# The transposes of the first expert's late token chunks, listed ahead of the third early second-pass chunk

## The chip, the cores and the metric

One core of one Trainium2 chip runs one launch of the kernel. The metric is device time in microseconds (us), the median of the timed runs of the whole launch. TensorE (PE in the rows) does matrix products, VectorE (DVE) and ScalarE (ACT) evict and split results, GpSimd (POOL) subtracts and issues gathers and scatters by index, SyncE (SP) issues the other loads. Each engine takes its instructions in the order of a list of its own, and the five lists wait for each other by semaphores.

## What is computed

```python
def reference(**kwargs):
    attn_out = _attn_ref(q, k, v)          # block-causal attention, 4 x 8 heads, 576 tokens, head size 64
    x = attn_out as 2304 tokens x 512
    x = _moe_ref(x, w1, w2, w3, w_out)     # max of three products, then one product back to 512
    return _moe2_ref(x, ...)               # 8 experts, the two best of each token

def _moe2_ref(x, w_gate, w_noise, noise, w1, w2):
    ...
    for e in range(E):
        for k in range(2):
            mask = top2[:, k] == e
            h = np.maximum(x[mask] @ w1[e], 0.0)
            out[mask] += top2_w[mask, k, None] * (h @ w2[e])
```

## The kernel before, in words

Attention and the first mixture layer fill the first half of the launch. This case lies in the second half, the eight experts. Every number is kept as a high and a low fp32r part, and a product takes three matmuls: high by high, low by high, high by low.

The tokens of an expert are packed into up to five chunks of 128 (chunks 0 to 4). For an expert `e` the steps are:

- `gather(e)`: one indirect DMA on POOL for each chunk brings 128 rows of `x2d` into a tile `xg` (L1078; 6 buffers, so a later gather waits until the transposes have read an earlier tile).
- `transposes(e, c0, c1)`: four transposes on PE for each chunk (L1096) into one PSUM bank, then ACT copies the bank to the high part `xh` (L1098) and DVE subtracts for the low part `xl` (L1099).
- `mm1(e, f, ...)`, the first pass: for each of 8 groups `f` of 128 hidden columns, four blocks of the depth by three matmuls (L1108 to L1110) into one PSUM bank; ACT evicts the high part (L1112), DVE the low part (L1113).
- `mm2(e, c, HT)`, the second pass: for each chunk 8 groups by three matmuls (L1156 to L1158); DVE scales the result into `y` (L1161, for the first expert L1163), and POOL scatters `y` to `out_rows` (L1164).

The weights of the next expert come in six pieces (`load_expert`): SP loads a piece into `rw` (2 buffers; L159 or L164), ACT copies the high part to `w` (L172), POOL subtracts the low part (L173). The subtraction is what gives `rw` back, so the load of piece 3 waits for the subtraction of piece 1, and so on.

The first expert is split. Its chunks 0 to 2 (`CE = 3`) are known early: they are transposed and pass `mm1` in 8 groups of 384 tokens while the last tokens are still being routed. Chunks 3 and 4 are gathered after that, and the program then lists the second pass of chunks 0, 1 and 2, the transposes of chunks 3 and 4, their `mm1` (8 groups of 256 tokens, 96 matmuls), the second pass of chunk 3, the five transposes of the next expert, the second pass of chunk 4, and then expert by expert. The banks of the transposes and of both passes come from `bank2()`, which takes a `b` and a `t` bank in turn, four buffers each.

The order on each engine is not the program's: a scheduler places the instructions by a simulated time line, and among those ready it goes by the place in the program. So ACT's list mixes the copies of weight pieces (L172), of transposes (L1098) and the evictions (L1112), and one that waits holds all that stand behind it.

Of the kernel before, what the change touches and what calls it, by code (L numbers as in the profile page):

```python
# [29 lines left out]
CE = 3  # L30
# [80 lines left out]
def plain(ap):  # L111
    return ap.bitcast(F32)
# [3 lines left out]
def tile_attention_moe_moe(ctx, tc, qT, kT, v, w1, w2, w3, w_out, gates, noise, e1, e2, out):  # L116
# [938 lines left out]
    def bank2():  # L1055
        turn[0] ^= 1
        if turn[0]:
            return ps2.tile([128, 512], F32, name="b")
        return psT.tile([128, 512], F32, name="t", bufs=4)
# [6 lines left out]
    def wt2(e, s, f):  # L1066
        g = f // 3
        o = (f - 3 * g) * 512
        return EW[e, 1, g][:, s, o:o + 512]
# [13 lines left out]
    def transposes(e, c0=0, c1=NCH):  # L1083
        if c0 == 0:
            XGT[e] = [mw.tile([128, 4, CAP], F32R, name=n) for n in ("xh", "xl")]
        th, tl = XGT[e]
        for c in range(c0, c1):
            if e == 0 and c < CE and BT:
                ps = ps2.tile([128, 512], F32, name="b")
            else:  # L1090
                ps = bank2()
            ps = ps.rearrange("p (k t) -> p k t", k=4)
            n = min(128, CAPS[e] - 128 * c)
            ps = ps[:, :, :n]
            for kt in range(4):
                nc.tensor.transpose(ps[:, kt], XG[e, c][:n, kt * 128:(kt + 1) * 128], ident[:n, :n])  # L1096
            s = slice(c * 128, c * 128 + n)
            nc.scalar.activation(th[:, :, s], ps, AF.Copy)  # L1098
            nc.vector.tensor_sub(tl[:, :, s], ps, plain(th[:, :, s]))  # L1099
# [39 lines left out]
    def mm2(e, c, HT):  # L1139
        n = min(128, CAPS[e] - 128 * c)  # L1140
        at, by = isc[:n, e, c:c + 1], idt[:n, e, c, 1:2]
        if e == 0 and c < CE:
            at, by = ise[:n, c:c + 1], ide[0][:n, c, 1:2]
        if e:
            prev = PREV[(e * NCH + c) % 2][:n]
            gi = nc.gpsimd.indirect_dma_start(
                out=prev, out_offset=None, in_=out,
                in_offset=bass.IndirectOffsetOnAxis(ap=at, axis=0),
                bounds_check=NTOK - 1, oob_is_err=False)
            for (ee, o) in osc:  # L1150
                if ee == e:
                    tc.declare_no_dep(gi.ins, o.ins, reason="rows of other tokens")
        ps = bank2()[:n]
        for f in range(8):
            a, l = (HT[f](s, c * 128, c * 128 + n) for s in range(2))
            nc.tensor.matmul(ps, a, wt2(e, 0, f), start=f == 0, stop=False)  # L1156
            nc.tensor.matmul(ps, a, wt2(e, 1, f), start=False, stop=False)  # L1157
            nc.tensor.matmul(ps, l, wt2(e, 0, f), start=False, stop=f == 7)  # L1158
        y = mw.tile([128, DM], F32, name="y", bufs=2)[:n]
        if e:  # L1160
            nc.vector.scalar_tensor_tensor(y, ps, by, prev, op0=OP.mult, op1=OP.add)  # L1161
        else:
            nc.vector.tensor_scalar(y, ps, by, None, op0=OP.mult)  # L1163
        st = nc.gpsimd.indirect_dma_start(  # L1164
            out=out, out_offset=bass.IndirectOffsetOnAxis(ap=at, axis=0),
            in_=y, in_offset=None, bounds_check=NTOK - 1, oob_is_err=False)
        for (ee, o) in osc:
            if ee == e:
                tc.declare_no_dep(st.ins, o.ins, reason="rows of other tokens")
        osc.append((e, st))  # L1170
# [86 lines left out]
    nc.vector.tensor_scalar(ig[:, 1:], idt[:, 1:, :, 0], float(NTOK - 1), None, op0=OP.min)  # L1257
    nc.vector.tensor_copy(isc[:, 1:], idt[:, 1:, :, 0])
    for c in range(CE):
        mm2(0, c, HT)  # L1260
    transposes(0, CE)
    for e in range(E):
        nw = weights_of(e + 1) if e + 1 < E else iter(())
        if e == 1:
# [121 lines left out]
```

## Time and profile before

| | |
|---|---|
| median of 3 runs | 1006.35 us (1005.23 to 1008.45) |
| the profiled execution, its own time | 1008.53 us |
| its span, first to last instruction | 1006.8 us |
| mean granted TensorE clock | 0.988 |
| PE busy | 978.2 us (97%) |
| DVE, ACT, POOL busy | 430.0, 398.1, 393.1 us |

The span is what the rows below are counted in, from its start; 1.73 us of the execution's time lie around it. The profiled execution is the slowest of the runs shown, 2.18 us above their median. PE is the busiest engine by far; the others have idle time of their own, which costs nothing as long as PE does not wait for it. In the rows, a group in square brackets at the end of a line is the idle time of the engine just before the instruction, and what ended it.

### The profile page before, as it was taken

How to read it: one execution, taken by the hardware profiler on the slowest of the kernel's cores; microseconds unless marked ns; L12 is line 12 of the kernel's file. 1: busy time of each engine (PE TensorE's matmuls, PEld its weight loads, DVE VectorE, ACT ScalarE, POOL GpSimd, SP SyncE). 2: the span in 40 equal slices, each digit the busy share in tenths (PEclk: the TensorE clock that was granted, in tenths of full speed). 3: DMA queues.
4: the chain of work that ended last, by engine and by line, in shares of the span. 5: the costliest groups of instructions: out<-in, count | busy, mean ns of one | idle time of the engine just before them, and what ended most of it. 6: DMA issues, size and time to landing. Idle time of an engine off the chain costs nothing. (4 is left out here: it accounts for less than half of the span.)

```text
span 1006.8 us, 17057 instructions
## 1 busy us (share of the span) xinstructions
PE 978.2 (97%) x6558; PEld 875.3 (87%) x6558; DVE 430.0 (43%) x1260; ACT 398.1 (40%) x934; POOL 393.1 (39%) x303
## 2 busy tenths in 40 slices
PE   8989998999999999999999799999999999999997
PEld 5876897999999899999999699898898989888895
DVE  6873556664567665743246322222222222221221
ACT  5586444654545545541124144232332414232210
POOL 2875120130302213121221477574756556574302
PEclk9999998999999999999999999999999999999999
DMA  8831315122112121302013456353534445342101
GB/s 267 289 125 52 109 38 196 51 54 64 36 44 70 55 63 41 84 23 98 22 33 126 148 162 208 115 177 105 160 107 154 146 138 171 106 165 84 61 12 57
DMA packets 75860, 106.15 MB, mean 105 GB/s; under 512 B 23548, under 2 KB 48124, under 8 KB 75776
## 3 DMA queue, kind: packets, MB, share of 16 engines
q1 hardware_dynamic: 63408, 75.97, 24.3%
q0 software_dynamic: 10192, 28.28, 8.6%
q10 hardware_dynamic: 2176, 0.79, 0.4%
q8 instruction: 52, 0.85, 0.4%
q14 instruction: 32, 0.26, 0.1%
HBM read 85.35 MB, written 20.53 MB: 105 GB/s over the span
## 5 line engine op out<-in xcount | busy, mean ns | idle before, releaser
L173 POOL TENSOR_TENSOR w<-rw,w 128x1536 fp32r<-128x1536 f32 (+1 forms) x42 | 131.6, 3138 | 74.2 <-ACT w L172 57.6
L752 POOL TENSOR_TENSOR hl<-hm,hh 128x512 fp32r<-128x512 f32 x21 | 27.4, 1303 | 175.6 <-ACT hh L751 174.5
L172 ACT ACTIVATE w<-rw 128x1536 fp32r<-128x1536 f32 (+1 forms) x42 | 56.4, 1344 | 81.4 <-issue 43.3
L1108 PE MATMUL b<-xh,w 128*128 128x384 f32 (+7 forms) x272 | 87.9, 323 | 0.5 <-DVE xB L1113 0.5
L1110 PE MATMUL b<-xh,w 128*128 128x384 f32 (+7 forms) x272 | 87.6, 322 | 0.0
L1109 PE MATMUL b<-xl,w 128*128 128x384 f32 (+7 forms) x272 | 87.5, 322 | 0.0
L736 PE MATMUL t<-xA,w 128*128 128x256 f32 x288 | 83.6, 290 | 0.0
L737 PE MATMUL t<-xA,w 128*128 128x256 f32 x288 | 82.5, 287 | 0.0
L738 PE MATMUL t<-xA,w 128*128 128x256 f32 x288 | 82.2, 285 | 0.0
L1108 PE MATMUL t<-xh,w 128*128 128x256 f32 x240 | 68.4, 285 | 5.1 <-ACT xh L1098 5.1
L265 POOL TENSOR_TENSOR Kl<-rk,Kh 128x576 fp32r<-128x576 f32 x16 | 23.0, 1439 | 123.8 <-ACT Kh L264 123.8
L1164 POOL DMA_INDIRECT out_rows<-y,isc x37 | 37.4, 1012 | 81.1 <-DVE y L1161 77.1
L1113 DVE SCALAR_TENSOR_TENSOR ht<-b,ht 128x384 fp32r<-128x384 f32 (+6 forms) x56 | 29.1, 520 | 92.7 <-ACT ht L1112 92.6
L1109 PE MATMUL t<-xl,w 128*128 128x256 f32 x240 | 67.8, 283 | 0.0
L1110 PE MATMUL t<-xh,w 128*128 128x256 f32 x240 | 67.8, 283 | 0.0
L1156 PE MATMUL b<-w,ht 128*128 128x512 f32 (+1 forms) x168 | 67.0, 399 | 0.0
L1158 PE MATMUL b<-w,ht 128*128 128x512 f32 (+1 forms) x168 | 66.4, 395 | 0.0
L1157 PE MATMUL b<-w,ht 128*128 128x512 f32 (+1 forms) x168 | 66.3, 394 | 0.0
L925 POOL DMA_INDIRECT ids<-rows,slots x36 | 35.7, 992 | 72.6 <-DVE slots L922 64.4
L736 PE MATMUL t<-xB,w 128*128 128x256 f32 x216 | 61.8, 286 | 0.0
L737 PE MATMUL t<-xB,w 128*128 128x256 f32 x216 | 61.3, 284 | 0.0
L738 PE MATMUL t<-xB,w 128*128 128x256 f32 x216 | 61.1, 283 | 0.0
(396 smaller groups left out, 2787.4 us busy)
## 6 DMA issues: line engine op xcount, KB each, us to landing
rw<-in_e SPq DMA_DIRECT2D x32, 768.0 KB
w<-in_w SPq DMA_DIRECT2D x18, 512.0 KB
rw<-in_e SPq DMA_DIRECT2D x16, 512.0 KB
rk<-in_kT SPq DMA_DIRECT2D x16, 288.0 KB
x2d<-x SPq DMA_DIRECT2D x18, 256.0 KB
out_rows<-x SPq DMA_DIRECT2D x9, 512.0 KB
w<-in_w_out SPq DMA_DIRECT2D x6, 512.0 KB
rq<-in_qT SPq DMA_DIRECT2D x16, 160.0 KB
```

Of the source, the lines that this page charges most:

```text
L172: nc.scalar.activation(t[:, 0, :c], r[:, :c], AF.Copy)
L173: nc.gpsimd.tensor_sub(t[:, 1, :c], r[:, :c], plain(t[:, 0, :c]))
L736: nc.tensor.matmul(ps[:, j], wh, x[:, 0], start=kt == 0, stop=False)
L737: nc.tensor.matmul(ps[:, j], wh, x[:, 1], start=False, stop=False)
L738: nc.tensor.matmul(ps[:, j], wl, x[:, 0], start=False, stop=kt == 3)
L1108: nc.tensor.matmul(p, wt1(e, 0, kt, f), th[:, kt, c0:c1], start=kt == 0, stop=False)
L1109: nc.tensor.matmul(p, wt1(e, 0, kt, f), tl[:, kt, c0:c1], start=False, stop=False)
L1110: nc.tensor.matmul(p, wt1(e, 1, kt, f), th[:, kt, c0:c1], start=False, stop=kt == 3)
L1156: nc.tensor.matmul(ps, a, wt2(e, 0, f), start=f == 0, stop=False)
L1157: nc.tensor.matmul(ps, a, wt2(e, 1, f), start=False, stop=False)
L1158: nc.tensor.matmul(ps, l, wt2(e, 0, f), start=False, stop=f == 7)
L1164: st = nc.gpsimd.indirect_dma_start(out=out, out_offset=bass.IndirectOffsetOnAxis(ap=at, axis=0), in_=y, in_offset=None, bounds_check=NTOK ...
```

## The change

```diff
     for c in range(CE):
+        if c == CE - 1:
+            transposes(0, CE)
         mm2(0, c, HT)
-    transposes(0, CE)
     for e in range(E):
```

The transposes of the first expert's chunks 3 and 4 are listed between the second pass of chunk 1 and that of chunk 2. Nothing is added or removed. The scheduler then also places other instructions anew.

PE, at the end of the second pass of chunk 1 (its bank is `t`) and the start of that of chunk 2 (bank `b`, first operand in `xB`); lines with + are of the change:

```order
 L1157 MATMUL t<-w,hl 128x512
 L1158 MATMUL t<-w,hh 128x512
+L1096 MATMUL b<-ident,xg 128x128 x4
+L1096 MATMUL t<-ident,xg 128x128 x4
 L1156 MATMUL b<-w,xB 128x512
 L1157 MATMUL b<-w,xB 128x512
```

The eight transposes now stand ahead of the 24 matmuls of chunk 2; in the kernel before they stand behind them.

ACT, from the last evictions of the early `mm1` (into `hm` and `hl`, 128x384) on. The 128x256 rows of L1112 are the evictions of the late `mm1`, groups 0, 1, 2 and so on. Before:

```order
L1112 ACTIVATE hl<-b 128x384
L172 ACTIVATE w<-rw 128x1536
L1098 ACTIVATE xh<-t 128x4x128
L172 ACTIVATE w<-rw 128x1536
L1098 ACTIVATE xh<-b 128x4x128
L1112 ACTIVATE hl<-t 128x256
L1112 ACTIVATE hh<-b 128x256
L1112 ACTIVATE hl<-t 128x256
L172 ACTIVATE w<-rw 128x1024
```

And in the changed kernel, one row further on:

```order
L1098 ACTIVATE xh<-b 128x4x128
L1098 ACTIVATE xh<-t 128x4x128
L172 ACTIVATE w<-rw 128x1536 x2
L1112 ACTIVATE hl<-t 128x256
L1112 ACTIVATE hh<-b 128x256
L1112 ACTIVATE hl<-t 128x256
L1112 ACTIVATE hx<-b 128x256
L1112 ACTIVATE x_6884<-t 128x256
L1112 ACTIVATE hx<-b 128x256
L172 ACTIVATE w<-rw 128x1024
L1112 ACTIVATE x_6916<-t 128x256
L1112 ACTIVATE hx<-b 128x256
```

Both copies of transposes now stand ahead of the first two weight pieces, and weight piece 3 has moved from behind group 2 to behind group 5. In both kernels pieces 4 and 5 follow group 7, and then come the five transpose copies of the next expert.

POOL, from the gathers of chunks 3 and 4 (the first row) on; L173 is the subtraction of a weight piece:

```order
 L1078 DMA xg<-x2d,ig 128x512 x2
 L1164 DMA out_rows<-y,ise 2304x512 x2
-L1078 DMA xg<-x2d,ig 128x512 x4
-L173 TENSOR_TENSOR w<-rw,w 128x1536
-L1078 DMA xg<-x2d,ig 128x512
+L1078 DMA xg<-x2d,ig 128x512 x6
+L173 TENSOR_TENSOR w<-rw,w 128x1536
 L1164 DMA out_rows<-y,ise 2304x512
-L1078 DMA xg<-x2d,ig 128x512
```

Two gathers of later experts, which use the `xg` tiles of chunks 3 and 4 again, have moved from behind the subtraction of weight piece 1 to ahead of it. On DVE the low part of chunk 3 now stands ahead of, and that of chunk 4 behind, the conversion of the other experts' index lists (L1257).

## Rows read from the trace of the kernel before

**Rows 1.** Waits of PE over the whole span: us in total, times, longest us

```profile
PE t L1108 <- ACT xh L1098: 5.1, 1, 5.1
```

**Rows 2.** Time line of PE: start us, us, instruction, count, [idle before <- what ended it]

```profile
566.38 0.39 PE L1156 MATMUL b<-w,xB 128*128 128x512 f32 x1
...
571.98 0.60 PE L1096 MATMUL t<-ident,xg 128*128 128x128 f32 x4
572.42 0.60 PE L1096 MATMUL b<-ident,xg 128*128 128x128 f32 x4
578.07 0.58 PE L1108 MATMUL t<-xh,w 128*128 128x256 f32 x1 [5.05 <-ACT xh L1098]
...
582.49 0.28 PE L1108 MATMUL b<-xh,w 128*128 128x256 f32 x1
...
591.54 0.39 PE L1156 MATMUL t<-w,hl 128*128 128x512 f32 x1
...
604.92 0.34 PE L1108 MATMUL b<-xh,w 128*128 128x384 f32 x1
```

**Rows 3.** Busy time by stretch; PEclk, the granted clock, stands third from the end

```profile
578.00:582.00 4.00, 3.93 (x18) 3.93 (x19) 0.69 (x1) 0.02 (x1) 3.23 (x4) 0.50 0.37 124
...
583.00:591.00 8.00, 8.00 (x70) 8.00 (x69) 2.51 (x7) 3.23 (x7) 5.90 (x2) 1.00 0.61 158
```

**Rows 4.** Time line of ACT at the transposes

```profile
573.93 1.48 ACT L172 ACTIVATE w<-rw 128x1536 fp32r<-128x1536 f32 x1 [18.17 <-DMA rw<-in_e]
...
576.05 1.48 ACT L172 ACTIVATE w<-rw 128x1536 fp32r<-128x1536 f32 x1
577.44 0.58 ACT L1098 ACTIVATE xh<-b 128x512 fp32r<-128x512 f32 x1
```

**Rows 5.** Gather of chunk 4 on POOL, then a stretch; its last number is GB/s

```profile
559.48 0.96 POOL L1078 DMA_INDIRECT xg<-x2d,ig  x1 [0.30 <-issue]
...
559.00:563.00 4.00, 4.00 (x19) 3.23 (x18) 2.16 (x10) 0.00 (x0) 1.89 (x3) 1.00 0.48 132
```

**Rows 6.** Time line of DVE: the conversion of the index lists

```profile
570.58 0.18 DVE L1257 TENSOR_SCALAR ig<-idt 128x35 int32<-128x35 f32 x1 [3.24 <-DMA idt<-ids]
```

**Rows 7.** Time line of POOL: a gather and three weight subtractions

```profile
574.84 0.95 POOL L1078 DMA_INDIRECT xg<-x2d,ig  x1 [0.30 <-issue]
575.80 3.46 POOL L173 TENSOR_TENSOR w<-rw,w 128x1536 fp32r<-128x1536 f32 x1
...
582.98 3.55 POOL L173 TENSOR_TENSOR w<-rw,w 128x1536 fp32r<-128x1536 f32 x1
...
586.49 2.41 POOL L173 TENSOR_TENSOR w<-rw,w 128x1024 fp32r<-128x1024 f32 x1
```

**Rows 8.** Weight pieces 3, 5 and 9: issue on SP's queue, copy on ACT

```profile
579.29 0.37 SPq L159 DMA_DIRECT2D rw<-in_e  x1
585.36 1.06 ACT L172 ACTIVATE w<-rw 128x1024 fp32r<-128x1024 f32 x1
...
594.28 1.49 ACT L172 ACTIVATE w<-rw 128x1536 fp32r<-128x1536 f32 x1 [0.77 <-DMA rw<-in_e]
...
615.18 0.37 SPq L159 DMA_DIRECT2D rw<-in_e  x1
...
618.80 1.06 ACT L172 ACTIVATE w<-rw 128x1024 fp32r<-128x1024 f32 x1 [0.54 <-DMA rw<-in_e]
```

**Rows 9.** Second expert's transposes: first and third copy on ACT, third subtraction on DVE

```profile
597.78 0.60 ACT L1098 ACTIVATE xh<-b 128x512 fp32r<-128x512 f32 x1 [2.01 <-PE b L1096]
...
598.75 0.60 ACT L1098 ACTIVATE xh<-b 128x512 fp32r<-128x512 f32 x1
...
599.61 0.68 DVE L1099 TENSOR_TENSOR xl<-b,xh 128x512 fp32r<-128x512 f32 x1
```

**Rows 10.** Third expert: its fifth weight subtraction on POOL, its first eviction on ACT

```profile
635.28 3.50 POOL L173 TENSOR_TENSOR w<-rw,w 128x1536 fp32r<-128x1536 f32 x1 [3.39 <-ACT w L172]
...
665.59 0.48 ACT L1112 ACTIVATE ht<-b 128x368 fp32r<-128x368 f32 x1 [1.72 <-PE b L1110]
```

## The prediction

> **What bounds the kernel now.** I read the page first (PE is busy 97% of the span), then the list of PE's waits over the whole span, and then the time lines around the one wait that stands out. The longest single wait of PE lies exactly where the change works: once, for 5.1 us, the first matmuls of the late first pass wait for a transpose copy on ACT [rows 1]. From there to the last matmul of the launch the list names no other wait of PE. So after this point the launch is as long as PE's list, and whatever PE gains here reaches the end, if nothing else then becomes late.
>
> The time line of PE shows the place. The second pass of chunk 2 runs from 566.38 to 571.98 (24 matmuls, 5.6 us, 0.70 for a group of three), the eight transposes follow it, the last four starting at 572.42, and PE stands from 573.02 to 578.07 [rows 2]. ACT shows why. It has been idle for 18.17 us, held by a weight piece whose load lands at 573.93; only behind that copy comes the first transpose copy, and behind a second weight copy (576.05) the second one at 577.44, which ends at 578.02 [rows 4]. The transposes had been ready since 573. PE did not wait for the copies' work, but for two weight loads that stood ahead of them in ACT's list.
>
> The pause costs a second time. [...]
>
> **The change, part by part.**
>
> *PE's work.* The eight transposes are the same eight, ahead of chunk 2 instead of behind it, so chunk 2 and the transposes together still end at 573.0. Cost nothing.
>
> *The wait removed.* The transposes now run at 566.4 to 567.4, when ACT has nothing to do until 573.93 [rows 4]. Two copies of 0.58 us are over by about 568.5. On DVE the low part of chunk 3 follows at once; that of chunk 4 stands behind the conversion of index lists, which runs at 570.58 when its load lands [rows 6], and is ready about 571.5, with 0.18 for that conversion, as much for the one behind it, and 0.7 for the subtraction. Both are before 573.0, so the late first pass starts without the wait: **5.05 us** [rows 2]. Chunk 2's 5.6 us are the cover for copies and subtractions; without it PE would wait for at least the last copy and subtraction, 0.58 + 0.68 = 1.3.
>
> *The clock.* The late first pass is 8 groups of 12, 96 matmuls, and runs from 578.07 to 591.54, 13.47 us. Until 582.49 stand 20 of them, 0.221 us each; from there to 591.54 the last 76, 0.119 each [rows 2]. At 0.119 throughout it would take 11.43. With no pause ahead of it there is no reason for the fall, so **2.04 us** more. Together 7.09.
>
> *What is queued behind the moved rows on ACT.* The eviction of group 0 now stands behind both weight copies. The second starts at 576.05 as before and ends at 577.53; PE is through with group 0 at about 573.0 + 12 x 0.119 = 574.4. Each of the eight groups has a bank of its own (four `b`, four `t`, the older users read long before), so PE does not wait for evictions inside this pass, and needs group 0 only when chunk 3's second pass starts, at 591.54 - 7.09 = 584.45. Groups 0 to 5 are evicted by 582. Cost nothing, with 6 us to spare.
>
> *Weight piece 3.* Groups 6 and 7 stand behind it. On POOL two more gathers stand ahead of the subtraction of piece 1: the four end at 575.79, two more take 2 x 1.25, so the subtraction moves from 575.80 to 578.3 and ends at 581.8 instead of 579.26 [rows 7]. It gives the buffer back; before, the load of piece 3 went out 0.03 behind it, at 579.29 [rows 8]. Now it goes out at 581.8. How long it takes isn't shown there (ACT came to it late). A load of the same size went out at 615.18 and was waited for until 618.80, 3.62 us; the copy at 585.36 bounds it at 6.07 from above [rows 8]. I take 3.62, since that one was waited for. It lands at 585.4, is copied by 586.5, and group 6 is evicted at 586.8, low part at 587.2. PE wants it at 584.45 + 6 x 0.70 = 588.65. Cost nothing; at 6.07 it would be 0.6.
>
> *Weight piece 5 and the next expert's transposes.* The subtraction of piece 2 starts at 582.98 as before, since the same work stands ahead of it. That of piece 3 takes 2.41 and needs the copy that ends at 586.5; it starts then, against 586.49 before [rows 7]. So piece 5 goes out at 588.9 again, and ACT has its copy at 594.28 again, waiting for the load [rows 8], while PE has come 7 us nearer. The five transpose copies of the next expert stand behind that copy. Before, they came at 597.78 and were then waited for by nobody [rows 9]. Now the first starts at 595.75 and the third ends at 597.3; the third low part starts 0.86 behind its copy and takes 0.68 [rows 9], so it ends at 598.25. PE reaches the next first pass at 604.92 - 7.09 = 597.83 [rows 2] and its first matmul with a low part some 0.35 later, for the scheduler has put two high ones first there. Cost 0.1. At the upper bound of piece 3 (6.07) everything behind it slips: copy until 588.9, piece 5 out at 591.3, at 596.7 on ACT after the 5.4 us that it took from 588.9, third low part at 600.6, a wait of 1.9. With the 0.6 above that is 2.5 us.
>
> [...] The row shows ACT idle for 18.17 us with a ready copy behind the one that waits [rows 4]. [...] If ACT could pass the waiting copy, the sum would be 7.09; since it can't, it is 7.0 and at worst 4.6.
>
> *Later.* Loads, gathers and scatters keep the order that they had, and each expert's sixth piece waits for PE's release of the last weights, so the chains fall in with PE again.
>
> **Sum.** 5.05 + 2.04 - 0.1 = 7.0 us. The profiled execution would have a span of 999.8 instead of 1006.8 and a time of 1001.5 instead of 1008.53; it was 2.18 above the median of the runs, so the median goes from 1006.35 to **999.4**. Bounds of the gain: 7.1 and 4.6. What a measurement of this kernel can tell from no change is about 0.3%, 3 us.
>
> **The rivals.**
>
> *The wait moves to the next expert.* Piece 3 or 5 lands later than I take it, and the transpose copies behind piece 5 hold PE at the next first pass. For it: ACT's list, and that ACT's copy at 594.28 does not come earlier with PE [rows 8]. Against: the load of the same size took 3.62. By the upper bound the gain is 4.6, time 1001.7; every us of lateness costs one.
>
> *Nothing reaches the end.* PE runs 7 us ahead, and the weight chain, which doesn't, stops it in the second or third expert. For it: POOL's subtractions are not moved by the gain at first. Against: the third expert's fifth subtraction ends at 638.78, and its first eviction comes at 665.59 [rows 10], over 20 us behind. Time 1006.3.
>
> *Slower: the transposes now hold the second pass of chunk 2.* PE's matmuls run in the order of the list, so a gather that is late at 566.4 now holds 5.6 us of matmuls that needed no gather; before, they covered it. The gather of chunk 4 is issued at 559.48 [rows 5] and both bring 0.52 MB (2 x 128 x 512 x 4 bytes). From 559 to 563 the transfers are 132 GB/s [rows 5], which is 0.53 MB. So they are there by 563, 3.4 us early. Each us of landing after 566.4 costs one; from 573.5 on the change loses. Landing at 577 would give 1009.9. I see nothing that would delay it by 10 us.
>
> That the change doesn't do what it says is excluded: the lists show the transposes and both copies moved.
>
> **How the numbers follow.** Forecast (gain 6 to 7.5) 0.76; the wait moves 0.15; nothing reaches the end 0.06; slower 0.03. The predicted time is the forecast's, 999.4. Low end: the full 7.1, and 1.2 for the spread of the runs (1005.23 to 1008.45 before), 998.0. High end: the gain of 4.6, and about 1, 1002.7. That leaves out the last two rivals and a part of the tails. Faster by over 0.3% (below 1003.3): the first two cases less 0.02 for a moved wait of over 4 us, 0.89. Within 0.3%: 0.06 and those 0.02, 0.08. Slower: 0.03.
>
> **What would show it.** In the changed profile PE should go from chunk 2 into the late first pass without a pause, at about 573; the granted clock should stay at 1.00 through 573 to 585; ACT's two transpose copies should stand near 567, ahead of the weight copies at 573.9 and 576; the first subtraction on POOL should start near 578.3 and the load of piece 3 go out near 581.8. Chunk 3's second pass should start near 584.5, the next expert's first pass near 598 with a wait of a few tenths at most on `xl`. A pause there of over 1 us shows the first rival, one later in an expert the second, one at 566.4 the third. My forecast is wrong if the clock falls all the same, or if the loads at 573.93 land at another time than in the execution that I read.

## The result, and the profile after

| | before | after |
|---|---|---|
| median, measured side by side | 1008.54 us, 8 runs (1005.23 to 1011.02) | 998.59 us, 8 runs (996.05 to 1003.97) |
| ratio after to before, 95% interval | | 0.9913 [0.9892, 0.9933] |
| the profiled execution, its span | 1008.53, 1006.8 | 998.79, 997.0 |
| mean granted clock | 0.988 | 0.992 |

The median fell by 10 us (6.8 to 10.9 by the interval of the ratio); the forecast was 7. To see which part of it is the change, one stretch is measured in every profile below: from the first matmul of the second pass of chunk 0 to the first matmul of the next expert's first pass. It took 604.92 - 555.11 = 49.81 us before and 595.03 - 552.48 = **42.55 us** after, 7.26 less. What follows it takes as long as before: 1006.8 - 604.92 = 401.9 and 997.0 - 595.03 = 402.0. The other 2.6 us by which the two spans differ lie ahead of the stretch (555.11 against 552.48), where the lists of all five engines are the same. So rows of after are to be read with 2.63 us added when they are put beside rows of before.

The waits of PE over the whole span, in the order of their length (us in total, times, longest). The row of [rows 1] is gone, and the longest wait that is left lies in the attention stage:

```profile
PE t L426 <- ACT xB L455: 2.5, 1, 2.5
PE s L317 <- DMA kve<-in_kT: 2.0, 1, 2.0
```

The time line of PE, answering to [rows 2]. The transposes stand ahead of chunk 2 (564.55), the late first pass (570.20) has no idle time in front of it and ends at 581.66, after 11.46 us instead of 13.47:

```profile
563.75 0.60 PE L1096 MATMUL b<-ident,xg 128*128 128x128 f32 x4
564.19 0.60 PE L1096 MATMUL t<-ident,xg 128*128 128x128 f32 x4
564.55 0.48 PE L1156 MATMUL b<-w,xB 128*128 128x512 f32 x1
...
570.20 0.28 PE L1108 MATMUL t<-xh,w 128*128 128x256 f32 x1
...
581.66 0.39 PE L1156 MATMUL t<-w,hl 128*128 128x512 f32 x1
...
595.03 0.51 PE L1108 MATMUL b<-xh,w 128*128 128x384 f32 x2
595.43 0.44 PE L1109 MATMUL b<-xl,w 128*128 128x384 f32 x1
...
597.46 0.28 PE L1108 MATMUL t<-xh,w 128*128 128x256 f32 x1
```

Busy time by stretch; the granted clock, third from the end, is 1.00 where [rows 3] had 0.50:

```profile
570.00:573.00 3.00, 3.00 (x26) 2.96 (x25) 0.75 (x1) 1.30 (x1) 2.39 (x3) 1.00 1.08 392
573.00:577.00 4.00, 4.00 (x36) 4.00 (x35) 1.24 (x4) 2.77 (x6) 3.36 (x4) 1.00 0.96 325
577.00:582.00 5.00, 5.00 (x43) 4.96 (x42) 1.04 (x3) 0.77 (x2) 4.81 (x3) 1.00 0.39 123
```

The time line of ACT, answering to [rows 4, 8]. Both transpose copies run the moment their transposes end, in the idle time that used to stand in front of the first weight copy; then ACT waits for the weights with nothing behind it that PE wants before 581.66. Group 0 is evicted at 575.37, piece 3 copied at 583.17, piece 5 at 591.49, each of the two after a wait for its load:

```profile
564.39 0.60 ACT L1098 ACTIVATE xh<-b 128x512 fp32r<-128x512 f32 x1 [11.26 <-PE b L1096]
564.88 0.59 ACT L1098 ACTIVATE xh<-t 128x512 fp32r<-128x512 f32 x1
571.70 1.49 ACT L172 ACTIVATE w<-rw 128x1536 fp32r<-128x1536 f32 x1 [6.22 <-DMA rw<-in_e]
573.97 1.49 ACT L172 ACTIVATE w<-rw 128x1536 fp32r<-128x1536 f32 x1 [0.78 <-DMA rw<-in_e]
575.37 0.36 ACT L1112 ACTIVATE hl<-t 128x256 fp32r<-128x256 f32 x1
...
583.17 1.06 ACT L172 ACTIVATE w<-rw 128x1024 fp32r<-128x1024 f32 x1 [3.80 <-DMA rw<-in_e]
584.13 0.36 ACT L1112 ACTIVATE x<-t 128x256 fp32r<-128x256 f32 x1
...
591.49 1.49 ACT L172 ACTIVATE w<-rw 128x1536 fp32r<-128x1536 f32 x1 [1.30 <-DMA rw<-in_e]
```

DVE: the low part of chunk 4, and much later the third low part of the next expert (its first and second stand at 593.49 and 594.10). They answer to [rows 6, 9]:

```profile
568.13 0.68 DVE L1099 TENSOR_TENSOR xl<-t,xh 128x512 fp32r<-128x512 f32 x1
...
594.70 0.68 DVE L1099 TENSOR_TENSOR xl<-b,xh 128x512 fp32r<-128x512 f32 x1
```

POOL and SP's queue, answering to [rows 7, 8]: the subtractions of pieces 1 and 3, and the issue of the load of piece 3, 0.03 behind the end of the former:

```profile
575.69 3.50 POOL L173 TENSOR_TENSOR w<-rw,w 128x1536 fp32r<-128x1536 f32 x1
...
584.31 2.41 POOL L173 TENSOR_TENSOR w<-rw,w 128x1024 fp32r<-128x1024 f32 x1 [0.39 <-ACT w L172]
```

```profile
579.22 0.37 SPq L159 DMA_DIRECT2D rw<-in_e  x1
```

### The profile page after: what moved, and what is told of

Its sections match the earlier page's. It is cut to its first block, busy times and chain, and to the rows that moved or that the text cites. A ratio compares the mean times of both kernels' runs of the same rounds, so it can differ in the third digit from the quotient of the medians.

```text
span 997.0 us, 17056 instructions
## 1 busy us (share of the span) xinstructions
PE 975.0 (98%) x6558; PEld 872.7 (88%) x6558; DVE 429.1 (43%) x1260; ACT 396.8 (40%) x934; POOL 393.1 (39%) x303
## 5 line engine op out<-in xcount | busy, mean ns | idle before, releaser
L173 POOL TENSOR_TENSOR w<-rw,w 128x1536 fp32r<-128x1536 f32 (+1 forms) x42 | 131.7, 3138 | 70.6 <-ACT w L172 55.1
```

The costliest lines, as they stand in the source:

```text
L173: nc.gpsimd.tensor_sub(t[:, 1, :c], r[:, :c], plain(t[:, 0, :c]))
```

## The experiments

Theory A is the prediction's: PE stood because two ready transpose copies were queued on ACT behind weight copies that waited for loads, and the pause cost once more through the granted clock. The rivals: that only the place of the transposes counts and not ACT's list; that the slow start of the late first pass has nothing to do with the pause; that the gathers limit how early the transposes may stand; and that part of the 10 us is chance. The table holds what all of them gave. "Stretch" is the one defined above, "late pass" is the late first pass, and "next group" the first group of the next expert's first pass (12 matmuls of 384 tokens), which shows a wait there.

| kernel | median, us | ratio to before, 95% | stretch | late pass | next group |
|---|---|---|---|---|---|
| before | | | 49.81 | 13.47 | 2.10 |
| after | 998.59 | 0.9913 [0.9892, 0.9933] | 42.55 | 11.46 | 2.43 |
| the change again (n1_after) | 1000.06 | 0.991 [0.9881, 0.9939] | 42.55 | 11.45 | 2.27 |
| before again (n0_same) | 1007.99 | 1.0003 [0.9984, 1.0021] | 49.86 | 13.43 | 2.10 |
| DVE copies (e1_dve) | 1002.09 | 0.9926 [0.99, 0.9952] | 44.37 | 11.90 | 2.09 |
| one chunk moved (e5_one) | 1008.43 | 0.9992 [0.9958, 1.0025] | 49.73 | 13.38 | 2.09 |
| 12 idle matmuls (e2_warm12) | 1008.16 | 0.9994 [0.9966, 1.0023] | 49.73 | 13.04 | 2.10 |
| 20 idle matmuls (e2b_warm20) | 1006.5 | 0.9992 [0.9974, 1.0011] | 48.16 | 11.56 | 2.09 |
| ahead of chunk 1 (e3_c1) | 1002.07 | 0.9942 [0.9915, 0.9969] | 43.44 | 11.45 | 2.27 |
| ahead of chunk 0 (e3_c0) | 1008.63 | 1.0012 [0.9995, 1.0029] | 50.70 | 11.46 | 2.09 |

The kernel before had a median of 1008.68 us (32 runs) beside n1_after, e1_dve, e5_one and e2_warm12, and of 1007.25 us (35 runs) beside the other four.

### Before and the change, each once more

Nothing is edited.

> The changed kernel again, beside fresh runs of the one before. Theory A (the gain is the wait on ACT and the half clock behind it, 7.1 us at the place of the change; what more the first comparison showed comes from the half of the launch ahead of the change, which differs from run to run): the profile goes from chunk 2 into the late first pass without a wait, and from the start of the second pass of chunk 1 to the end of the launch it is 7.0 to 7.3 us shorter than the profile of before; the stage ahead of that may be longer or shorter by up to 3 us. Theory B (the change shortens something else too, 9 to 10 us in all): the stage ahead of the second pass of chunk 1 is again 2 to 3 us shorter than before.

> The kernel before again, with nothing changed. The stretch from chunk 0's second pass to the next expert's first pass takes 49.8 us within 0.1, as in the profile of before, and the ratio is 1.000. What lies ahead of the stretch may differ by up to 3 us from the profile of before. Rival (part of the 10 us by which the two profiled executions differ lies in the stretch itself and was chance): the stretch is shorter than 49.5.

The stretch is the steady part: 42.55 and 42.55 with the change, 49.81 and 49.86 without. What stands ahead of it is not. ACT's last conversion of a key tile in the attention stage (L264) starts at 419.39 in the kernel before, at 416.88 in the changed one, and at 417.36 in the kernel before taken again; nothing in the lists differs there. So the 2.63 us by which the changed kernel's profile arrives early at the stretch are no part of the change: the second profile of the change reaches the stretch at 553.91, the second of the kernel before at 553.05, and theory B's 2 to 3 us are not there again. From the second pass of chunk 1 to the end of the launch it is 446.25 and 446.21 us without the change, 439.08 and 438.95 with it, 7.2 to 7.3 less, as theory A had it (7.0 to 7.3). What makes the attention stage shorter or longer stays open; its granted clock varies too (from 60 to 120 us and from 120 to 180 us 0.94 and 0.94 before, 0.89 and 1.00 in the changed kernel, 0.97 and 0.94 in the kernel before taken again).

### The copies on DVE, everything else where it was

Is it ACT's list? Here the transposes stay behind chunk 2, and only the two copies go to DVE, which waits for no weights. An edit of the kernel before:

```diff
-            nc.scalar.activation(th[:, :, s], ps, AF.Copy)
+            nc.vector.tensor_copy(th[:, :, s], ps) if e == 0 and c >= CE else nc.scalar.activation(th[:, :, s], ps, AF.Copy)
```

> The order of before, with the high parts of chunks 3 and 4 of the first expert copied by DVE instead of ACT. Theory A (PE waited for copies that stood behind two waiting weight copies in ACT's list): the transposes end at about 573, DVE copies twice and subtracts twice, PE waits about 1.2 us for the copies and some tenths for the low part, and the clock stays; 5 to 5.5 us faster than before. Rival (the time comes from having the transposes themselves ahead of chunk 2, not from ACT's list): PE waits near 5 us as before, no gain.

PE, DVE and ACT at the place. ACT is stuck behind the same load, idle for 18.28 us, and it no longer matters: the two copies (DVE prints them as CAST) start within 0.5 us of the end of their transposes, PE stands for 1.17 us, no longer for 5.05, and the granted clock stays at 1.00.

```profile
573.10 0.39 PE L1108 MATMUL t<-xh,w 128*128 128x256 f32 x1 [1.17 <-DVE xh L1098]
```

```profile
572.00:575.00 3.00, 1.81 (x13) 1.61 (x14) 2.23 (x4) 1.49 (x1) 2.37 (x4) 1.00 1.08 395
575.00:585.00 10.00, 10.00 (x86) 10.00 (x85) 2.69 (x7) 4.68 (x9) 9.21 (x5) 1.00 0.60 209
```

```profile
571.76 0.68 DVE L1098 CAST xh<-t 128x512 fp32r<-128x512 f32 x1
572.36 0.68 DVE L1098 CAST xh<-b 128x512 fp32r<-128x512 f32 x1
```

```profile
572.95 1.49 ACT L172 ACTIVATE w<-rw 128x1536 fp32r<-128x1536 f32 x1 [18.28 <-DMA rw<-in_e]
```

The stretch is 5.44 us shorter without moving a transpose, inside the 5 to 5.5 that theory A gave. The 1.8 us that the change has over it are the 1.17, 0.44 in the late pass (11.90 against 11.46; its low parts come while it runs) and 0.2 ahead of the pass: there the transposes stand behind chunk 2 and count to their end (571.93), while in the changed kernel the next matmul starts before that. The 1.17 is the price of copies with no cover, which the prediction had put at 1.3 (0.58 + 0.68).

### Only chunk 3 moved

If one copy stays behind the weights, is anything gained? An edit of the kernel before:

```diff
+        if c == CE - 1:
+            transposes(0, CE, CE + 1)
         mm2(0, c, HT)
-    transposes(0, CE)
+    transposes(0, CE + 1)
```

> Half of the change: the transposes of chunk 3 ahead of chunk 2, those of chunk 4 behind it as before. The list of ACT then has the copy of chunk 3 ahead of both weight copies and that of chunk 4 behind both. Theory A: the last copy still ends at about 578 on the scale of before, PE waits about 5 us as before (a little more, since PE reaches it earlier by nothing), the clock falls; a gain of 0 to 0.5 us. Rival (each set of transposes moved out of the way brings its share): 3.5 us faster.

```profile
566.60 0.60 ACT L1098 ACTIVATE xh<-b 128x512 fp32r<-128x512 f32 x1 [11.26 <-PE b L1096]
573.54 1.48 ACT L172 ACTIVATE w<-rw 128x1536 fp32r<-128x1536 f32 x1 [6.34 <-DMA rw<-in_e]
575.64 1.48 ACT L172 ACTIVATE w<-rw 128x1536 fp32r<-128x1536 f32 x1 [0.62 <-DMA rw<-in_e]
577.03 0.58 ACT L1098 ACTIVATE xh<-b 128x512 fp32r<-128x512 f32 x1
```

The copy of chunk 3 runs at 566.60, that of chunk 4 at 577.03 behind both weight copies, and PE stands for 5.07 us as before. The matmuls of a group take both chunks at once, so the later copy sets the start: half of the move is worth nothing. The rival's 3.5 us are not there.

### Idle matmuls in the pause

Does the pause slow the late pass? Idle bf16 matmuls fill part of it, with the wait for the copy untouched. An edit of the kernel before, first with 12, then with 20:

```diff
-    transposes(0, CE)
+    transposes(0, CE); warm(psT.tile([128, 512], F32, name="t", bufs=4), 12)
```

> The order of before, with 12 idle matmuls of 128x512 (their result is read by nothing) behind the transposes of chunks 3 and 4, about 2.6 us of PE work inside the wait. Theory A (the pause of 5 us costs a second time, by the half clock behind it): the late first pass starts when it did before, its first 20 matmuls take 0.12 instead of 0.22 us, and the launch is 2.0 us faster than before. Rival (the first 20 matmuls are slow for another reason, such as the loads at that time): they stay slow, the same time as before.

PE and the granted clock with 12. They end at 576.76, PE stands for another 2.81 us, and the clock falls although PE is at work again by then:

```profile
574.01 2.75 PE L135 MATMUL t<-ones 128*128 128x512 bf16 x12
...
579.58 0.39 PE L1108 MATMUL t<-xh,w 128*128 128x256 f32 x1 [2.81 <-ACT xh L1098]
```

```profile
579.00:580.00 1.00, 0.42 (x3) 0.42 (x4) 0.44 (x1) 0.52 (x2) 1.00 (x1) 1.00 0.36 131
580.00:581.00 1.00, 1.00 (x10) 1.00 (x9) 0.25 (x1) 0.00 (x0) 0.86 (x2) 0.86 0.00 0
581.00:584.00 3.00, 3.00 (x16) 3.00 (x16) 0.42 (x1) 0.38 (x1) 2.39 (x3) 0.50 0.83 280
```

The late pass takes 13.04 us, 0.43 less, and starts 0.35 later in the stretch (23.31 us behind its start, against 22.96). The expected 2.0 us did not come: 12 are too few. That left open whether the pause or something else slows the late pass, so the pause was made shorter still.

> Order of before, with 20 idle matmuls behind the transposes, where 12 still left PE standing for 2.8 us and gained nothing. 20 take about 4.4 us and leave a pause of 0.6 to 1.2 us. Theory (the pause costs a second time through the granted clock): the clock stays at 1.00, the late first pass takes 11.4 us instead of 13.47, and the stretch 47.8 instead of 49.81, 2.0 us faster, with the wait for the transpose copy itself untouched. Rival (the slow start of the late first pass has another cause, such as the weights or the type of the operands): it takes 13 us again and nothing is gained.

```profile
572.55 4.48 PE L135 MATMUL t<-ones 128*128 128x512 bf16 x20
578.02 0.38 PE L1108 MATMUL t<-xh,w 128*128 128x256 f32 x1 [0.99 <-ACT xh L1098]
```

```profile
578.00:582.00 4.00, 3.98 (x33) 3.98 (x34) 1.11 (x2) 0.69 (x2) 3.23 (x4) 1.00 0.47 146
```

With a pause of 0.99 us the clock stays at 1.00 in the stretch where [rows 3] have 0.50, and the late pass takes 11.56 us instead of 13.47, with the same weights and operands, and starting behind the same late copy. The stretch gains 1.65, not 1.91, because the late pass started 0.25 us later in it (578.02 - 554.81 = 23.21 against 578.07 - 555.11 = 22.96). On the kernel's time 1.65 us cannot be told from nothing; the trace alone shows them. It is a remedy for the clock alone, and the change leaves no pause for it to fill.

### Earlier still

How much room has the change? In the program the transposes go ahead of chunk 1, then of chunk 0. In PE's list the scheduler leaves only the four of chunk 3 there and places those of chunk 4 behind (565.72 and 566.08), so it is chunk 3's gather that PE meets. Edits of the changed kernel:

```diff
-        if c == CE - 1:
+        if c == CE - 2:
             transposes(0, CE)
```

> The transposes of chunks 3 and 4 stand one chunk earlier than in the change, at the start of the second pass of chunk 1. Theory (the gathers' landing sets how early the transposes may stand; they are there by about 562 to 563 on the time line of the kernel before): PE reaches them at about 561 and stands for 1 to 2 us inside chunk 1, the granted clock stays at 1.00, and from chunk 0's second pass to the next expert's first pass the launch is 5 to 6 us shorter than before, instead of 7.26. Rival (the gathers have landed long before): no wait, 7.2 us as with the change.

```profile
562.18 0.66 PE L1096 MATMUL t<-ident,xg 128*128 128x128 f32 x4 [0.66 <-DMA xg<-x2d,ig]
...
565.72 0.60 PE L1096 MATMUL b<-ident,xg 128*128 128x128 f32 x4
```

```profile
558.72 0.98 POOL L1078 DMA_INDIRECT xg<-x2d,ig  x1 [3.48 <-DVE sq L1232]
```

PE meets the landing of chunk 3's gather: it stands for 0.66 us (expected 1 to 2), until 3.46 us behind the gather's start on POOL. The stretch is 43.44, so 6.37 us are gained, more than the 5 to 6 expected and less than with the change. The mechanism is theory A's, the size of the wait was put too high.

```diff
-        if c == CE - 1:
+        if c == 0:
             transposes(0, CE)
```

> The transposes stand at the very start of the second passes, ahead of nearly all matmuls that could cover the gathers. This makes the prediction's slower rival happen on purpose. Theory: PE reaches the first transpose at about 555.3 and stands for 6 to 7 us until its gather lands near 562; the granted clock falls behind that pause as it did in the kernel before, for about 2 us more; the stretch takes as long as before, 49.8 us within 1.5, and the kernel's time is that of before. Rival (the gathers land early): 7.2 us faster, as the change.

```profile
559.33 1.08 PE L1096 MATMUL b<-ident,xg 128*128 128x128 f32 x4 [6.34 <-DMA xg<-x2d,ig]
...
566.08 0.60 PE L1096 MATMUL t<-ident,xg 128*128 128x128 f32 x4
```

```profile
555.78 0.98 POOL L1078 DMA_INDIRECT xg<-x2d,ig  x1 [3.42 <-DVE sq L1232]
```

```profile
557.00:559.00 2.00, 0.00 (x0) 0.00 (x0) 1.02 (x7) 0.00 (x0) 0.96 (x1) 0.50 0.52 147
559.00:563.00 4.00, 3.67 (x11) 3.11 (x12) 0.69 (x1) 0.60 (x1) 0.00 (x0) 0.50 0.22 61
```

This is the mechanism of the prediction's slower rival, brought about by the edit. PE stands for 6.34 us from 552.99 on (the stretch counts from there), until 3.55 us behind the start of chunk 3's gather; the clock falls while it stands, and the stretch is 50.70, 0.89 us longer than before. The late pass is fast and starts without a wait, and all that it saves is lost at the new place. Expected were 49.8 within 1.5.

## Why the prediction was right

*The wait removed, 5.05.* The transposes at 563.75 (566.38 by the time of before), both copies by 565.5, chunk 4's low part until 568.81, the late pass without a pause at 570.20: by the time of before at 572.83, where 573.0 was forecast. 5.05 and another 0.19: chunk 2 and the transposes took 6.64 us before (566.38 to 573.02, where the last transposes end) and take 6.45 now (563.75 to 570.20), since the next matmul starts before the last transposes have ended (564.55 against 564.19 + 0.60). That it was ACT's list, and not the transposes' place as such, is shown by the copies on DVE: 5.44 us gained with the transposes where they had been.

*The clock, 2.04.* The late pass took 11.46 where 11.43 was forecast, 2.01 less than before. That the pause is the cause is shown by the 20 idle matmuls: with 0.99 us of it left the clock stays at 1.00 and the pass takes 11.56. In the kernel before the clock falls while PE stands (1.00 from 574 to 575, 0.81 in the next microsecond, 0.50 from 576 to 578), and behind the pause of 5.05 us the work starts at 0.50 [rows 3]; so it does behind the 6.34 us with the transposes ahead of chunk 0. Behind 2.81 us (12 idle matmuls) it starts at 1.00 and falls to 0.50 a little over 1 us later; behind 0.99 us (20 idle matmuls) and 1.17 us (DVE copies) it stays at 1.00.

*The rows queued behind on ACT, nothing.* Group 0 was evicted at 575.37, by the time of before at 578.0; PE did not wait in the pass, and needed it at 581.66.

*Piece 3, nothing.* POOL began the subtraction at 575.69, by the time of before at 578.32 (forecast 578.3). The load went out at 579.22 and was copied at 583.17: 3.95 us where 3.62 was taken, the one duration that was too small. Group 6 was evicted at 584.13, its low part was ready at 584.96, and its first matmul of chunk 3's second pass stands at 585.85: 0.9 us to spare, where the forecast had 1.45 (587.2 against 588.65).

*The new wait, 0.1.* Piece 5's copy came at 591.49, by the time of before at 594.12, forecast 594.28. The third low part ended at 595.38 (598.01, forecast 598.25), and its matmul started at 595.43. The first group of the next expert took 2.43 us instead of 2.10, and 2.27 in the second profile of the change, so the wait is 0.2 to 0.3 and was put too low. Little of it can be seen at the end: from the start of that pass to the end of the span it is 401.97 and 401.84 with the change, 401.88 and 401.79 without. The first rival, which had up to 2.5 us lost behind the late weights, is not what happened. A version that makes piece 5 later by a known time wasn't tried, so the price of such lateness stays argued.

*The sum.* 5.05 + 0.19 + 2.01 = 7.25 inside the stretch, where 7.26 was measured, and 7.31 by the second pair of profiles; less 0.1 or so behind it, and the forecast was 7.0. The time forecast, 999.4, was taken from a median of 1006.35, and the kernel before showed 1008.54, 1008.68 and 1007.25 in longer comparisons; the changed kernel 998.59 and 1000.06. That 999.4 came out 0.8 us from 998.59 is in part luck: the median that it started from was 2.2 us low, and the medians differ by 2.95 more than the 7.0 that was taken off. The ratios leave 6.8 to 10.9 us in the one comparison (0.0067 and 0.0108 of 1008.54) and 6.2 to 12.0 in the other, and 7.2 lies in both. The differences of the medians, 9.95 and 8.62, exceed the stretch's by 2.7 and 1.4 us; whether that belongs to the change is not shown. No row of the stretch or of what follows has it: in the ten profiles the stretch starts between 552.48 and 556.27, with lists that are the same, and what follows it takes 401.8 to 402.0 in all of them. In other comparisons the medians miss the stretch both ways: 6.6 against 5.44 for the DVE copies, 5.2 against 6.37 for the transposes ahead of chunk 1.

*The rivals.* Nothing stopped PE later: the list of waits has no entry behind the place. The gathers were there in time. In the profile of before, POOL's DMA queue moved 0.52 MB, the size of both, between 559.4 and 563.05, and the transposes of chunk 4 would have come at 566.8: 3.8 us to spare. The prediction read the same time from the traffic of all queues, which does not say whose bytes they are; the two landings of chunk 3's gather that PE met, 3.46 and 3.55 us behind the gather's start, agree with it.

## What to carry to other kernels

When PE waits for a short copy, look at what stands ahead of the copy on its engine, and not at how long the copy takes: 0.58 us of work was 4.4 us late (ready at 573.0, started at 577.44) because an instruction ahead of it waited for a load. What it waited for had not even been issued for most of that time: ACT stood idle from 555.76 on, and in the time line of SP's queue the first two weight pieces go out at 569.37 and 570.02, behind seven small loads of index lists (561.49 to 568.86). Whether these loads could be listed ahead of the index lists, and what that would give, no run shows. The remedy that the runs show is to put the copy's source early enough that the scheduler lists it ahead of the load's user, or to give the copy to an engine that does not wait for that load (DVE, 5.44 us of the stretch); and all copies that one matmul needs have to move, since the last one sets its start (with one of the two moved PE still stood for 5.07 us). How far it may be moved up is set by its own input: two chunks earlier the same edit turned 7.3 us of gain in the stretch into 0.9 of loss.

## What was not expected of the hardware

The clock can fall after the pause is over: behind 2.81 us of standing, PE had been at work for over a microsecond when the granted clock went from 1.00 to 0.50 (580 to 581 us, 0.86 in that row), and the late pass was slow for it. So filling about half of the pause bought 0.43 us in the pass and nothing in the stretch, while filling all but 0.99 us of it bought 1.91 in the pass. That the length of the pause alone decides it is doubtful. In the attention stage PE stands once for 2.50 us, until 168.74, in the changed kernel, and the granted clock is 1.00 all through from 120 to 180; in the kernel before it stands there for 3.52 us, until 168.20, and the clock is 0.50 from 170 to 176. With 12 idle matmuls the same wait is 2.5 us long, as in the changed kernel, but from ACT's eviction into `xA` behind it (L440) to the next one into `Ph` (L375), which waits for PE, it takes 7.59 us (169.91 to 177.50), against 5.31 in the changed kernel (169.65 to 174.96) and 7.84 in the kernel before (169.11 to 176.95). That speaks for a fall of the clock there too; it is the author's estimate from these times. No run was made to find what else may decide. And the launch varies by more ahead of the place than most edits are worth: the stretch starts between 552.48 and 556.27 in the ten profiles, and the eight runs of the changed kernel go from a span of 994.3 us at a mean granted clock of 0.995 to 1002.2 at 0.987. Two single runs would have told little of a size of 1 to 2 us.
